# Fused attention and two mixers: where scores and products change from native fp32 to split halves

## The chip, the core and the metric

The kernel runs on one core of a Trainium2 chip. The metric is device time in microseconds. The kernel before takes 890.24 us (median of 3 runs, 889.29 to 891.47); its profiled execution took 888.24 us.

The engines are named as in the profile: PE multiplies matrices (its weight loads are PEld), DVE is the vector engine, ACT the scalar engine, POOL is GpSimd, SP issues most transfers.

## The reference

Three stages follow one another: causal attention over 4 batches, 12 heads, 448 positions and 64 columns; a mixer over positions and then channels; and a second mixer with a cosine and a sine in it.

```
scores = scale * q @ k.T ; scores = where(causal mask, -1e9, scores)
attn   = exp(scores - max) ; attn = attn / (sum(attn) + 1e-9)
x      = attn @ v                                # heads side by side: 768 columns

h  = relu(x.T @ w_tok1) @ w_tok2 ; u = x + h.T   # 448 -> 256 -> 448
x  = u + relu(u @ w_ch1) @ w_ch2                 # 768 -> 1536 -> 768

theta = x @ w_theta ; zr, zi = x * cos(theta), x * sin(theta)
u  = x + w_tok_r @ zr + w_tok_i @ zi
out = u + relu(u @ w_ch)
```

q, k and v are 32-bit floats. The weights reach the kernel as 64-bit floats and are turned into 32-bit ones on the chip.

## The kernel before, in words

Attention runs over 24 pairs of heads (4 batches with 6 pairs each, numbered 0 to 23), each pair in 7 tiles: tile (0, 0) holds the first 64 positions of both heads, and tiles (i, h) for i = 1 to 3 hold 128 queries of head h against 192, 320 or 448 keys. The 168 tiles are the steps of the main loop. `scores` (L332) multiplies q by k into a bank of PSUM, lets DVE add the mask and find the largest value (L356), and lets ACT take the exponential and its sum (L358). Four steps later (`LAG`) `pv` (L384) multiplies the probabilities by v, and after a pair's last tile `finish` (L406) divides by the sums.

Two tables of pair numbers choose how precisely a product is made. A pair in `NATIVE` (L30; pairs 0 to 7) multiplies q and k as they are, in fp32: the 64 rows of each head dimension are loaded into the upper half of a tile and POOL clears the other half (L275). The other pairs load q and k twice over both halves, and ACT and DVE split each into a rounded high part and a rest (L290 to L296): q's high part and rest lie one above the other in `qs`, and `scores` multiplies them by `kh` (L349) and `kl` (L351). A pair in `NATPV` (L31; pairs 0 to 11) has its probabilities transposed by PE (L365), copied by ACT (L367), and multiplied by v in fp32 (L393). The other pairs have the probabilities split into two fp16 halves by ACT and DVE (L376, L378), transposed by a DMA (L381), and multiplied in three fp16 products per block (L403); for these, v is scaled and split too, by `value_squares` and `value_split` (L303, L308), during the pair before.

Beside the pairs runs the conversion of weights. `fetch64` brings a 64-bit tile; `abs64` (L175) lets ACT take the absolute value of the high words with a changed exponent; `round64` (L178) lets DVE shift that left by three (L183), put the sign bit in (L184) and the low word's top bits (L185). 24 large and 4 small tiles are converted at steps given by `ROUNDINGS`; each is then scaled and split by POOL and DVE, and stored. Six tiles (`convert_late`) and the tables of the last mixer (`load_resident`) come later, through the same functions.

From step 53 on, units of the channel mixer (`run_units`, the products at L230 to L232 in `mm3`) are put between the steps by the table `UNIT_STEPS`. A scheduler orders the instructions of each engine; `high_priority` and `issue_after` steer it. Each engine then runs its own list in order, and waits where an operand is missing.

Of the kernel before, what the change touches and what calls it, by code (L numbers as in the profile page):

```python
# [54 lines left out]
def fused(ctx, tc, q, k, v, w_tok1, w_tok2, w_ch1, w_ch2, w_theta, w_tok, w_ch, out):  # L55
# [327 lines left out]

    def pv(pp, i, h):  # L384
        if pp.ps is None:
            pp.ps = bank("pv", 1)
        reg = 0 if i == 0 else ((i - 1) * 2 + h + 1) * D
        pt = pp.pts[i, h]
        if pp.native_pv:
            blks = [8] if i == 0 else [6 + h] + [2 * u + h for u in range(i)]  # L390
            n = D if i == 0 else 2 * D
            for u, vt in enumerate(blks):
                pp.pv = nc.tensor.matmul(pp.ps[:, reg:reg + n], lhsT=pt[:, u], rhs=pp.v[0][:, vt * D:vt * D + n],  # L393
                                 start=(u == 0), stop=(u == len(blks) - 1))
            return
# [10 lines left out]
    def finish(pp, xb, xg):  # L406
        ps, sm = pp.ps, pp.sm
        nc.vector.tensor_scalar(out=sm[:, 0:7], in0=sm[:, 0:7], scalar1=1e-9, scalar2=pp.unit, op0=ALU.add, op1=ALU.mult)
        nc.vector.reciprocal(out=sm[:, 0:7], in_=sm[:, 0:7])
        nc.vector.tensor_tensor(out=xb[:, 1:4, :].rearrange("p i (h d) -> p (i h) d", h=2),  # L410
                                in0=ps[:, D:7 * D].rearrange("p (j d) -> p j d", d=D),
                                in1=sm[:, 0:6].unsqueeze(2).to_broadcast([P, 6, D]), op=ALU.mult)
        for h in range(2):
            r = slice(64 * h, 64 * h + 64)
            nc.vector.tensor_scalar(out=xb[r, 0, 64 * h:64 * h + 64], in0=ps[r, 0:D],
                                    scalar1=sm[r, 6:7], scalar2=None, op0=ALU.mult)
# [570 lines left out]
```

## Time and profile before

| | us |
|---|---|
| median of 3 runs | 890.24 (889.29 to 891.47) |
| profiled execution | 888.24 |
| its span, first to last instruction | 886.5 |
| PE busy | 851.7 (96%) |
| PE weight loads busy | 547.8 (62%) |
| DVE busy | 632.8 (71%) |
| ACT busy | 544.0 (61%) |
| POOL busy | 166.3 (19%) |

Busy time is the union of an engine's instructions. Matmuls overlap, so the time that one takes from the engine is the distance between two starts, not its listed duration; a native fp32 matmul appears as two. The last product of probabilities and v starts at 508.6 us; the second mixer follows.

### The profile page before, as it was taken

What the parts mean: (1) busy time and instruction counts of PE and PEld (TensorE: products, weight loads), DVE (VectorE), ACT (ScalarE), POOL (GpSimd) and SP (SyncE); (2) the same over time, 40 slices, a digit from 0 to 9 for tenths busy, and PEclk for the clock granted to TensorE, in tenths of its full rate; (3) what the DMA queues carried; (4) which work ended last, traced back from release to release, by engine and by line L of the source; (5) the groups of instructions that cost most, each with busy time, mean ns of one, the idle gap of its engine ahead of it and who ended that gap; (6) DMA issues with size and microseconds to landing.
All of it is one profiled execution on the core that took longest, in us unless ns stands there. A gap on an engine that the chain in (4) does not pass through costs nothing.

```text
span 886.5 us, 16065 instructions
## 1 busy us (share of the span) xinstructions
PE 851.7 (96%) x5619; PEld 547.8 (62%) x5619; DVE 632.8 (71%) x1511; ACT 544.0 (61%) x1271; POOL 166.3 (19%) x319
## 2 busy tenths in 40 slices
PE   7999889999899999999999999999999999999998
PEld 6888767776656566565666554555555555555554
DVE  6899996878998775766886258768856448567442
ACT  6798776757776564657655257437746447466441
POOL 2232232223251200121211112051111002101000
PEclk9999989999999999999999999999999999999999
DMA  7857865747899996656565778711622132231011
GB/s 217 255 182 228 289 231 183 272 169 232 205 310 306 288 210 148 165 202 129 162 186 137 232 240 293 238 55 41 201 62 67 50 116 67 69 116 58 18 50 73
DMA packets 105793, 149.63 MB, mean 169 GB/s; under 512 B 61104, under 2 KB 72304, under 8 KB 105712
## 3 DMA queue, kind: packets, MB, share of 16 engines
q1 hardware_dynamic: 105168, 147.59, 55.3%
q0 software_dynamic: 384, 0.79, 0.4%
q8 instruction: 44, 0.72, 0.3%
q14 instruction: 37, 0.30, 0.1%
q10 hardware_dynamic: 160, 0.23, 0.1%
HBM read 112.39 MB, written 22.81 MB: 153 GB/s over the span
## 4 chain that ended last, share of the span: by engine, by line
PE 66%; DVE 13%; DMA 11%; issue 4%; ACT 3%; POOL 1%; SPq 1%; ACTq 0%; DVEq 0%; POOLq 0%
PE ps_mm L230 15%; PE ps_mm L231 15%; PE ps_mm L232 15%; DMA pt<-ph 6%; PE ps_pv L393 3%; PE ps_sc L349 3%; PE ps_sc L230 3%; PE ps_sc L231 3%; PE ps_sc L232 3%; DVE sb L356 2%; DVE ph L378 1%; PE ps_mm L365 1%; DVE wf L184 1%; DMA ws<-w_c 1%; DVE wf L185 1%
## 5 line engine op out<-in xcount | busy, mean ns | idle before, releaser
L230 PE MATMUL ps_mm<-h,ws 128*128 128x448 f16 x432 | 151.9, 353 | 0.4 <-DMA ws<-w_c 0.4
L231 PE MATMUL ps_mm<-h,ws 128*128 128x448 f16 x432 | 152.2, 353 | 0.0
L232 PE MATMUL ps_mm<-h,ws 128*128 128x448 f16 x432 | 152.2, 353 | 0.0
L230 PEld LDWEIGHTS <-ws 128*128 128x128 f16 x720 | 70.4, 98 | 63.4 <-issue 4.1
L232 PEld LDWEIGHTS <-ws 128*128 128x128 f16 x720 | 70.4, 98 | 62.8 <-issue 3.1
L231 PEld LDWEIGHTS <-ws 128*128 128x128 f16 x720 | 70.5, 98 | 62.4 <-issue 4.2
L358 ACT ACTIVATE sb<-sb,mx 128x192 f32<-128x192 f32 (+3 forms) x168 | 89.2, 532 | 32.1 <-DVE mx L356 30.6
L230 PE MATMUL ps_mm<-ut,ws 128*128 128x448 f16 x288 | 102.0, 355 | 5.6 <-ACT ut L160 2.3
L231 PE MATMUL ps_mm<-ut,ws 128*128 128x448 f16 x288 | 102.0, 354 | 0.6 <-DVE ut L196 0.5
L232 PE MATMUL ps_mm<-ut,ws 128*128 128x448 f16 x288 | 102.1, 354 | 0.0
L356 DVE CUSTOM_DVE_ANT_0 sb<-ps_sc,mask 128x192 f32<-128x192 f32 (+3 forms) x168 | 74.3, 456 | 12.7 <-PE ps_mm L365 9.5
L124 ACT ACTIVATE junk<-acc 128x448 bf16<-128x448 f32 x72 | 41.1, 571 | 63.9 <-DVE acc L879 41.0
L160 ACT ACTIVATE ph<-sb 128x192 f16<-128x192 f32 (+3 forms) x84 | 36.4, 442 | 45.9 <-DMA pt<-ph 45.8
L393 PE MATMUL ps_pv<-v_raw,ptf 128*128 128x128 f32 (+1 forms) x456 | 63.9, 277 | 0.3 <-PE ps_mm L138 0.2
L378 DVE SCALAR_TENSOR_TENSOR ph<-sb,ph 128x64 f16<-128x64 f32 (+3 forms) x156 | 44.6, 328 | 26.4 <-ACT ph L160 26.2
L393 PEld LDWEIGHTS ps_pv<-v_raw,ptf 128*128 128x128 f32 x456 | 59.2, 193 | 5.0 <-PE ps_mm L138 1.5
L163 POOL TENSOR_SCALAR h<-t 128x448 f16<-128x448 f32 x48 | 32.8, 685 | 140.3 <-ACT t L477 140.1
L349 PE MATMUL ps_sc<-kh,qs 128*128 128x256 f32 (+2 forms) x112 | 45.9, 416 | 3.3 <-DVE mx L356 3.3
L230 PE MATMUL ps_sc<-th,ut 128*128 128x384 f16 x144 | 46.9, 326 | 0.0
L232 PE MATMUL ps_sc<-th,ut 128*128 128x384 f16 x144 | 46.8, 326 | 0.0
L231 PE MATMUL ps_sc<-th,ut 128*128 128x384 f16 x144 | 46.6, 326 | 0.0
L479 DVE TENSOR_TENSOR h<-t,h 128x448 f16<-128x448 f32 x48 | 30.2, 633 | 19.7 <-POOL h L163 19.5
(215 smaller groups left out, 2040.5 us busy)
## 6 DMA issues: line engine op xcount, KB each, us to landing
ws<-w_c SPq DMA_DIRECT2D x120, 384.0 KB, 4.5
raw<-in_w_ch_dram SPq DMA_DIRECT2D x30, 768.0 KB, 4.5
w_c<-ws SPq DMA_DIRECT2D x30, 384.0 KB, 3.5
q_raw<-in_q_dram SPq DMA_DIRECT2D x16, 448.0 KB, 4.1
k_raw<-in_k_dram SPq DMA_DIRECT2D x16, 448.0 KB, 4.9
v_raw<-in_v_dram SPq DMA_DIRECT2D x24, 288.0 KB, 3.2
x2d<-acc SPq DMA_DIRECT2D x24, 224.0 KB, 3.7
acc<-x2d SPq DMA_DIRECT2D x24, 224.0 KB, 2.8
```

The costliest lines, as they stand in the source:

```text
L124: nc.scalar.activation(j[:, 0:src.shape[-1]], src, AF.Square, accum_out=dst)
L160: nc.scalar.activation(dst, src, AF.Copy, scale=scale)
L163: e.tensor_scalar(out=dst, in0=src, scalar1=scale, scalar2=0.0, op0=ALU.mult, op1=ALU.add)
L230: nc.tensor.matmul(ps, lhsT=ka(a[:, 0]), rhs=kb(b[:, 0]), start=first, stop=False)
L231: nc.tensor.matmul(ps, lhsT=ka(a[:, 0]), rhs=kb(b[:, 1]), start=False, stop=False)
L232: return nc.tensor.matmul(ps, lhsT=ka(a[:, 1]), rhs=kb(b[:, 0]), start=False, stop=last)
L349: nc.tensor.matmul(ps[:, 0:n], lhsT=lhs, rhs=cut(pp.kh), start=True, stop=pp.kl is None)
L356: pp.first = nc.vector.tensor_tensor_reduce(out=dst, in0=src, in1=msk, op0=ALU.add, op1=ALU.min, scale=-0.125, scalar=3.0e38, accum_out=pp ...
L358: pp.last = nc.scalar.activation(sb[:, 0:kk], sb[:, 0:kk], AF.Exp, bias=pp.mx[:, j:j + 1], scale=-1.0, accum_out=pp.sm[:, j:j + 1])
L378: nc.vector.scalar_tensor_tensor(out=dst, in0=sb[:, c0:c1], scalar=PSC, in1=hi[:, c0:c1], op0=ALU.mult, op1=ALU.subtract)
L393: pp.pv = nc.tensor.matmul(pp.ps[:, reg:reg + n], lhsT=pt[:, u], rhs=pp.v[0][:, vt * D:vt * D + n], start=(u == 0), stop=(u == len(blks) - 1))
L479: gates[0] = nc.vector.tensor_tensor(out=t[:, 1], in0=f, in1=t[:, 0], op=ALU.subtract)
```

## The change

Four edits, all in the attention stage and in the conversion of weights:

- `NATIVE` grows to the pairs 0 to 11, and `NATPV` shrinks to 0 to 7. So pairs 8 to 11 turn round: their scores become native, and their probabilities and v are split.
- `abs64` no longer takes the absolute value: ACT copies with the same scale, and POOL multiplies the high words by zero in place, which leaves the sign bit alone. `round64` then shifts and puts the sign in with one DVE instruction instead of two.
- The products of tile (0, 0) are written twice, side by side (`twice`), the sums move by two columns, and `finish` makes all eight blocks of 64 columns with one multiplication. Before it, POOL multiplies a table `own` (a one for the rows of a head, a zero elsewhere) by the factor of tile (0, 0), which takes the place of two instructions of 64 rows. The clearing of a part of `x0` and `x1` is dropped.
- A native product of the last tile is 64 columns wide instead of 128, since the region behind it ends.

```
--- before.py
+++ after.py
@@ -27,8 +27,8 @@
 NEG = -1.0e30
 PSC = 32768.0
 BUFS = dict(ut=12, h2=8, acc=12, ws=8, wf=3, raw=3, sb=3, ph=3, pt=5, t=3, junk=1)
-NATIVE = {0, 1, 2, 3, 4, 5, 6, 7}
-NATPV = {0, 1, 2, 3, 4, 5, 6, 7, 8, 9, 10, 11}
+NATIVE = {0, 1, 2, 3, 4, 5, 6, 7, 8, 9, 10, 11}
+NATPV = {0, 1, 2, 3, 4, 5, 6, 7}
 AHEAD, LAG, LOOK = 500, 4, 2
 KEEP, UBACK = 6, 16
 ROUND_BITS, ROUND_FETCH, ROUND_SPLIT, ROUND_STORE = 1, 2, 3, 5
@@ -173,15 +173,16 @@
         nc.sync.dma_start(out=raw[:, :src.shape[-1]].rearrange("p n w -> p (n w)"), in_=src.bitcast(U32))
 
     def abs64(f, raw):
-        nc.scalar.activation(f, raw[:, :f.shape[-1], 1].bitcast(F32), AF.Abs, scale=REBIAS)
+        high = raw[:, :f.shape[-1], 1].bitcast(F32)
+        nc.scalar.activation(f, high, AF.Copy, scale=REBIAS)
+        product(high, high, 0.0, 1.0)
 
     def round64(f, raw):
 
 
-        low, high = raw[:, :f.shape[-1], 0], raw[:, :f.shape[-1], 1]
+        low, sign = raw[:, :f.shape[-1], 0], raw[:, :f.shape[-1], 1]
         u = f.bitcast(U32)
-        nc.vector.tensor_scalar(out=u, in0=u, scalar1=3, scalar2=None, op0=ALU.logical_shift_left)
-        nc.vector.scalar_tensor_tensor(out=u, in0=high, scalar=0x80000000, in1=u, op0=ALU.bitwise_and, op1=ALU.bitwise_or)
+        nc.vector.scalar_tensor_tensor(out=u, in0=u, scalar=3, in1=sign, op0=ALU.logical_shift_left, op1=ALU.bitwise_or)
         nc.vector.scalar_tensor_tensor(out=u, in0=low, scalar=29, in1=u, op0=ALU.logical_shift_right, op1=ALU.bitwise_or)
 
     def wf_tile():
@@ -239,6 +240,10 @@
     nc.gpsimd.memset(mask, 0.0)
     nc.gpsimd.affine_select(out=mask[:, 320:448], in_=mask[:, 320:448], compare_op=ALU.is_ge, fill=NEG,
                             base=0, pattern=[[-1, P]], channel_multiplier=1)
+    own = ac.tile([P, 2], F32, tag="own", name="own")
+    nc.vector.memset(own, 0.0)
+    for h in range(2):
+        nc.vector.memset(own[64 * h:64 * h + 64, h:h + 1], 1.0)
     mask0 = ac.tile([P, 2, 64], F32, tag="mask0", name="mask0")
     nc.vector.tensor_copy(mask0.rearrange("p a b -> p (a b)"), mask[:, 320:448])
     nc.vector.memset(mask0[64:128, 0, :], NEG)
@@ -262,7 +267,6 @@
     xbufs = []
     for j in range(2):
         xb = ac.tile([P, 4, P], F32, tag=f"x{j}", name=f"x{j}")
-        nc.gpsimd.memset(xb[:, 0, :], 0.0)
         xbufs.append(xb)
 
     loads = {}
@@ -325,7 +329,7 @@
             self.qs, self.kh, self.kl, self.v = parts[:4]
             self.unit = parts[4] if len(parts) > 4 else 1.0
             self.mx = ap2.tile([P, 7], F32, tag="mx", name="mx")
-            self.sm = ap2.tile([P, 8], F32, tag="sm", name="sm")
+            self.sm = ap2.tile([P, 10], F32, tag="sm", name="sm")
             self.pts, self.ps, self.sent = {}, None, None
             self.native_pv = b * NPR + pr in NATPV
 
@@ -356,7 +360,7 @@
         pp.first = nc.vector.tensor_tensor_reduce(out=dst, in0=src, in1=msk, op0=ALU.add, op1=ALU.min, scale=-0.125,
                                        scalar=3.0e38, accum_out=pp.mx[:, j:j + 1])
         pp.last = nc.scalar.activation(sb[:, 0:kk], sb[:, 0:kk], AF.Exp, bias=pp.mx[:, j:j + 1], scale=-1.0,
-                             accum_out=pp.sm[:, j:j + 1])
+                             accum_out=pp.sm[:, 2 + j:3 + j])
         if pp.native_pv:
             nt = 1 + i
             c0 = 64 if i == 0 else 0
@@ -381,16 +385,20 @@
         pp.sent = nc.sync.dma_start_transpose(out=pt[:, 0:nb, :], in_=ph[:, 0:nb * P])
         pp.pts[i, h] = pt
 
+    def twice(ap):
+        return ap.unsqueeze(1).to_broadcast([P, 2, D])
+
     def pv(pp, i, h):
         if pp.ps is None:
             pp.ps = bank("pv", 1)
-        reg = 0 if i == 0 else ((i - 1) * 2 + h + 1) * D
+        reg = 0 if i == 0 else ((i - 1) * 2 + h + 2) * D
         pt = pp.pts[i, h]
         if pp.native_pv:
             blks = [8] if i == 0 else [6 + h] + [2 * u + h for u in range(i)]
-            n = D if i == 0 else 2 * D
             for u, vt in enumerate(blks):
-                pp.pv = nc.tensor.matmul(pp.ps[:, reg:reg + n], lhsT=pt[:, u], rhs=pp.v[0][:, vt * D:vt * D + n],
+                n = 2 * D if reg < 7 * D else D
+                rhs = twice(pp.v[0][:, vt * D:(vt + 1) * D]) if i == 0 else pp.v[0][:, vt * D:vt * D + n]
+                pp.pv = nc.tensor.matmul(pp.ps[:, reg:reg + n], lhsT=pt[:, u], rhs=rhs,
                                  start=(u == 0), stop=(u == len(blks) - 1))
             return
         if i == 0:
@@ -400,20 +408,17 @@
             for u in range(i):
                 jobs += [(1 + u, 0, 2 * u + h), (1 + u, 1, 2 * u + h), (1 + i + u, 0, 2 * u + h)]
         for n, (blk, c, vt) in enumerate(jobs):
-            pp.pv = nc.tensor.matmul(pp.ps[:, reg:reg + D], lhsT=pt[:, blk], rhs=pp.v[c][:, vt * D:(vt + 1) * D],
+            rhs = pp.v[c][:, vt * D:(vt + 1) * D]
+            pp.pv = nc.tensor.matmul(pp.ps[:, reg:reg + (2 * D if i == 0 else D)], lhsT=pt[:, blk], rhs=twice(rhs) if i == 0 else rhs,
                              start=(n == 0), stop=(n == len(jobs) - 1))
 
     def finish(pp, xb, xg):
         ps, sm = pp.ps, pp.sm
-        nc.vector.tensor_scalar(out=sm[:, 0:7], in0=sm[:, 0:7], scalar1=1e-9, scalar2=pp.unit, op0=ALU.add, op1=ALU.mult)
-        nc.vector.reciprocal(out=sm[:, 0:7], in_=sm[:, 0:7])
-        nc.vector.tensor_tensor(out=xb[:, 1:4, :].rearrange("p i (h d) -> p (i h) d", h=2),
-                                in0=ps[:, D:7 * D].rearrange("p (j d) -> p j d", d=D),
-                                in1=sm[:, 0:6].unsqueeze(2).to_broadcast([P, 6, D]), op=ALU.mult)
-        for h in range(2):
-            r = slice(64 * h, 64 * h + 64)
-            nc.vector.tensor_scalar(out=xb[r, 0, 64 * h:64 * h + 64], in0=ps[r, 0:D],
-                                    scalar1=sm[r, 6:7], scalar2=None, op0=ALU.mult)
+        nc.vector.tensor_scalar(out=sm[:, 2:9], in0=sm[:, 2:9], scalar1=1e-9, scalar2=pp.unit, op0=ALU.add, op1=ALU.mult)
+        nc.vector.reciprocal(out=sm[:, 2:9], in_=sm[:, 2:9])
+        product(sm[:, 0:2], own, sm[:, 8:9], 1.0)
+        nc.vector.tensor_tensor(out=xb.rearrange("p i (h d) -> p (i h) d", h=2), in0=ps.rearrange("p (j d) -> p j d", d=D),
+                                in1=sm[:, 0:8].unsqueeze(2).to_broadcast([P, 8, D]), op=ALU.mult)
         pr2 = pp.pr % 2
         c = slice(pr2 * P, (pr2 + 1) * P)
         copy_to(pick("xhi"), xg[0][:, :, c], xb)
```

The first place is the native and split work on PE around the scores of 320 and 448 columns of a pair among 8 to 11. `ptf` are probabilities transposed by PE, `pt` by a DMA; `kh`, `kl`, `qs` are split halves, `k_pad` and `q_raw` native ones. Before:

```order
L349 MATMUL ps_sc<-kh,qs 128x320
L351 MATMUL ps_sc<-kl,qs 128x320
L393 MATMUL ps_pv<-v_raw,ptf 128x128 x3
L365 MATMUL ps_mm<-ident,sb_182 128x128 x2
L393 MATMUL ps_pv<-v_raw,ptf 128x128
L136 LDWEIGHTS ones
L136 MATMUL ps_mm<-tiny,ones 128x1
L138 LDWEIGHTS ones
L138 MATMUL ps_mm<-sqb,ones 128x1
L349 MATMUL ps_sc<-kh,qs 128x448
L351 MATMUL ps_sc<-kl,qs 128x448
L393 MATMUL ps_pv<-v_raw,ptf 128x128 x4
```

And now, where each product has its own weight load:

```order
L412 LDWEIGHTS pt
L412 MATMUL ps_pv<-v_hi,pt 128x64
L412 LDWEIGHTS pt
L412 MATMUL ps_pv<-v_raw,pt 128x64
L412 LDWEIGHTS pt
L412 MATMUL ps_pv<-v_hi,pt 128x64
L353 MATMUL ps_sc<-k_pad,q_raw 128x448 x2
L353 MATMUL ps_sc<-k_pad,q_raw 128x128
L136 LDWEIGHTS ones
L136 MATMUL ps_mm<-tiny,ones 128x1
L412 LDWEIGHTS pt
L412 MATMUL ps_pv<-v_hi,pt 128x64
```

The transposes by PE and the `kl` products are gone from here; runs of fp16 products of 64 columns, three a block, stand between native scores.

The second place is the list of POOL in the first pairs, where the weight tables `ws` are scaled (`g` is a power of two that DVE makes, `raw` the 64-bit words). Before:

```order
L275 MEMSET k_pad_668 64x896
L275 MEMSET q_raw_667 64x896
L130 TENSOR_SCALAR p_w10_141<-g_518 128x1
L130 TENSOR_SCALAR s_514<-g_518 128x1
L163 TENSOR_SCALAR ws_513<-wf_444,s_514 128x768
L130 TENSOR_SCALAR p_w10_141<-g_644 128x1
L130 TENSOR_SCALAR s_640<-g_644 128x1
L163 TENSOR_SCALAR ws_639<-wf_500,s_640 128x768
```

And now:

```order
L279 MEMSET k_pad_668 64x896
L279 MEMSET q_raw_667 64x896
L130 TENSOR_SCALAR p_w10_141<-g_519 128x1
L130 TENSOR_SCALAR raw_405<-raw_405 128x768
L130 TENSOR_SCALAR s_515<-g_519 128x1
L130 TENSOR_SCALAR sm_436<-own_177,sm_436 128x2
L163 TENSOR_SCALAR ws_514<-wf_445,s_515 128x768
L130 TENSOR_SCALAR p_w10_141<-g_645 128x1
L130 TENSOR_SCALAR s_641<-g_645 128x1
L163 TENSOR_SCALAR ws_640<-wf_501,s_641 128x768
```

A sign operation on `raw` stands between the two operations on `g`, and the one on the sums `sm` ahead of the scaling.

The third place is DVE's list at the same tiles: the bits of the weight tile `wf_635` and the sums of pair 2. Before:

```order
L127 TENSOR_SCALAR g_518<-g_518 128x1
L408 TENSOR_SCALAR sm_435<-sm_435 128x7
L409 RECIPROCAL sm_435<-sm_435 128x7
L183 TENSOR_SCALAR wf_635<-wf_635 128x768
L184 SCALAR_TENSOR_TENSOR wf_635<-raw_404,wf_635 128x768
L196 SCALAR_TENSOR_TENSOR ws_513<-wf_444,s_514,ws_513 128x768
L185 SCALAR_TENSOR_TENSOR wf_635<-raw_404,wf_635 128x768
L432 SCALAR_TENSOR_TENSOR h1_543<-ps_mm_544,h1_543 128x256
```

And now:

```order
L127 TENSOR_SCALAR g_519<-g_519 128x1
L417 TENSOR_SCALAR sm_436<-sm_436 128x7
L418 RECIPROCAL sm_436<-sm_436 128x7
L185 SCALAR_TENSOR_TENSOR wf_635<-wf_635,raw_405 128x768
L186 SCALAR_TENSOR_TENSOR wf_635<-raw_405,wf_635 128x768
L197 SCALAR_TENSOR_TENSOR ws_514<-wf_445,s_515,ws_514 128x768
L437 SCALAR_TENSOR_TENSOR h1_543<-ps_mm_544,h1_543 128x256
L437 SCALAR_TENSOR_TENSOR h1_543<-ps_mm_559,h1_543 128x256
```

The tile has two instructions on its bits instead of three, and the first of them reads `raw_405`, which POOL writes. The multiplication that reads POOL's two columns of `sm_436` follows 18 rows behind the reciprocal.

## Rows read from the trace of the kernel before

**Rows 1.** Busy time by stretch: us, each engine, granted clock, DMA share, GB/s
```profile
22.00:110.00 88.00, 83.88 (x602) 72.19 (x599) 81.45 (x208) 72.53 (x197) 25.24 (x41) 1.00 0.74 238
110.00:132.00 22.00, 18.71 (x109) 14.02 (x110) 19.91 (x46) 16.83 (x39) 8.21 (x14) 0.84 0.66 232
132.00:198.00 66.00, 65.99 (x459) 51.20 (x458) 50.41 (x120) 43.38 (x109) 15.96 (x29) 1.00 0.58 206
198.00:264.00 66.00, 61.46 (x462) 40.92 (x460) 63.32 (x162) 49.26 (x120) 24.96 (x42) 1.00 0.87 251
264.00:330.00 66.00, 61.11 (x480) 40.02 (x478) 51.52 (x152) 41.92 (x112) 10.44 (x16) 1.00 1.01 267
330.00:550.00 220.00, 212.31 (x1528) 131.88 (x1527) 146.61 (x380) 125.14 (x303) 35.25 (x73) 1.00 0.67 190
```

**Rows 2.** Timeline of PE in pair 9: start us, us, engine, line
```profile
149.30 0.39 PE L349 MATMUL ps_sc<-kh,qs 128*128 128x320 f32 x1
149.53 0.32 PE L351 MATMUL ps_sc<-kl,qs 128*128 128x320 f32 x1
149.69 0.27 PE L365 MATMUL ps_mm<-ident,sb 128*128 128x128 f32 x1
149.80 1.06 PE L393 MATMUL ps_pv<-v_raw,ptf 128*128 128x128 f32 x8
150.61 0.45 PE L349 MATMUL ps_sc<-kh,qs 128*128 128x448 f32 x1
150.90 0.36 PE L351 MATMUL ps_sc<-kl,qs 128*128 128x448 f32 x1
151.10 0.36 PE L230 MATMUL ps_mm<-ut,ws 128*128 128x448 f16 x1
```

**Rows 3.** Timeline of PE in pairs 1 to 3: native scores and what follows
```profile
24.44 0.49 PE L349 MATMUL ps_sc<-k_pad,q_raw 128*128 128x192 f32 x2
24.77 0.83 PE L393 MATMUL ps_pv<-v_raw,ptf 128*128 128x128 f32 x6
...
30.93 0.92 PE L349 MATMUL ps_sc<-k_pad,q_raw 128*128 128x448 f32 x2
31.68 0.49 PE L365 MATMUL ps_mm<-ident,sb 128*128 128x128 f32 x3
```

**Rows 4.** Timeline of PE around pair 16: ten fp16 products and what follows
```profile
305.31 0.19 PE L403 MATMUL ps_pv<-v_raw,pt 128*128 128x64 f16 x1
...
305.60 0.37 PE L349 MATMUL ps_sc<-kh,qs 128*128 128x256 f32 x1
```

**Rows 5.** Groups by line on DVE: count | busy us, mean ns | idle before
```profile
L378 DVE SCALAR_TENSOR_TENSOR ph<-sb,ph 128x64 f16<-128x64 f32 (+3 forms) x156 | 44.6, 328 | 26.4 <-ACT ph L160 26.2
...
L184 DVE SCALAR_TENSOR_TENSOR wf<-raw,wf 128x768 uint32<-128x768 uint32 (+2 forms) x34 | 33.8, 994 | 0.4
...
L183 DVE TENSOR_SCALAR wf<-wf 128x768 uint32<-128x768 uint32 (+2 forms) x34 | 21.8, 642 | 1.4 <-ACT wf L176 1.4
...
L167 DVE TENSOR_TENSOR qs<-q_raw,qs 64x896 fp32r<-64x896 f32 x16 | 17.9, 1117 | 0.5
...
L415 DVE TENSOR_SCALAR x<-ps_pv,sm 64x64 f32<-64x64 f32 x48 | 13.4, 279 | 0.4
L410 DVE TENSOR_TENSOR x<-ps_pv,sm 128x384 f32<-128x384 f32 x24 | 13.3, 552 | 1.3 <-PE ps_mm L439 0.7 <-PE ps_pv L403 0.4
...
L317 DVE SCALAR_TENSOR_TENSOR v_raw<-v_raw,sv,v_hi 128x576 f16<-128x576 f32 x12 | 11.1, 922 | 1.0 <-POOL v_hi L163 1.0
```

**Rows 6.** Timeline, POOL and DVE at 37 us: start us, us, engine, line
```profile
37.48 1.14 POOL L163 TENSOR_SCALAR ws<-wf,s 128x768 f16<-128x768 f32 x1
...
37.88 1.54 DVE L184 SCALAR_TENSOR_TENSOR wf<-raw,wf 128x768 uint32<-128x768 uint32 x1
```

**Rows 7.** Waits of the whole span: us in total, times, longest
```profile
PEld L403 <- DMA pt<-ph: 9.2, 14, 1.3
...
DVE ws L196 <- POOL ws L163: 6.9, 7, 1.4
```

More of the change, by code (lines that the diff above doesn't have):

```diff
@@ L175, in abs64 @@
     def abs64(f, raw):
-        nc.scalar.activation(f, raw[:, :f.shape[-1], 1].bitcast(F32), AF.Abs, scale=REBIAS)
+        high = raw[:, :f.shape[-1], 1].bitcast(F32)
+        nc.scalar.activation(f, high, AF.Copy, scale=REBIAS)
+        product(high, high, 0.0, 1.0)
     def round64(f, raw):
-        low, high = raw[:, :f.shape[-1], 0], raw[:, :f.shape[-1], 1]
+        low, sign = raw[:, :f.shape[-1], 0], raw[:, :f.shape[-1], 1]
         u = f.bitcast(U32)
-        nc.vector.tensor_scalar(out=u, in0=u, scalar1=3, scalar2=None, op0=ALU.logical_shift_left)
-        nc.vector.scalar_tensor_tensor(out=u, in0=high, scalar=0x80000000, in1=u, op0=ALU.bitwise_and, op1=ALU.bitwise_or)
+        nc.vector.scalar_tensor_tensor(out=u, in0=u, scalar=3, in1=sign, op0=ALU.logical_shift_left, op1=ALU.bitwise_or)
         nc.vector.scalar_tensor_tensor(out=u, in0=low, scalar=29, in1=u, op0=ALU.logical_shift_right, op1=ALU.bitwise_or)
@@ L241, in fused @@
                             base=0, pattern=[[-1, P]], channel_multiplier=1)
+    own = ac.tile([P, 2], F32, tag="own", name="own")
+    nc.vector.memset(own, 0.0)
+    for h in range(2):
+        nc.vector.memset(own[64 * h:64 * h + 64, h:h + 1], 1.0)
     mask0 = ac.tile([P, 2, 64], F32, tag="mask0", name="mask0")
@@ L382, in scores, with twice @@
         pp.pts[i, h] = pt
+    def twice(ap):
+        return ap.unsqueeze(1).to_broadcast([P, 2, D])
     def pv(pp, i, h):
@@ L390, in pv @@
             blks = [8] if i == 0 else [6 + h] + [2 * u + h for u in range(i)]
[L391 removed]
             for u, vt in enumerate(blks):
[L393 removed]
+                n = 2 * D if reg < 7 * D else D
+                rhs = twice(pp.v[0][:, vt * D:(vt + 1) * D]) if i == 0 else pp.v[0][:, vt * D:vt * D + n]
+                pp.pv = nc.tensor.matmul(pp.ps[:, reg:reg + n], lhsT=pt[:, u], rhs=rhs,
                                  start=(u == 0), stop=(u == len(blks) - 1))
@@ L402, in pv @@
         for n, (blk, c, vt) in enumerate(jobs):
-            pp.pv = nc.tensor.matmul(pp.ps[:, reg:reg + D], lhsT=pt[:, blk], rhs=pp.v[c][:, vt * D:(vt + 1) * D],
+            rhs = pp.v[c][:, vt * D:(vt + 1) * D]
+            pp.pv = nc.tensor.matmul(pp.ps[:, reg:reg + (2 * D if i == 0 else D)], lhsT=pt[:, blk], rhs=twice(rhs) if i == 0 else rhs,
                              start=(n == 0), stop=(n == len(jobs) - 1))
@@ L407, in finish @@
         ps, sm = pp.ps, pp.sm
[L408 to L416, printed above, removed]
+        nc.vector.tensor_scalar(out=sm[:, 2:9], in0=sm[:, 2:9], scalar1=1e-9, scalar2=pp.unit, op0=ALU.add, op1=ALU.mult)
+        nc.vector.reciprocal(out=sm[:, 2:9], in_=sm[:, 2:9])
+        product(sm[:, 0:2], own, sm[:, 8:9], 1.0)
+        nc.vector.tensor_tensor(out=xb.rearrange("p i (h d) -> p (i h) d", h=2), in0=ps.rearrange("p (j d) -> p j d", d=D),
+                                in1=sm[:, 0:8].unsqueeze(2).to_broadcast([P, 8, D]), op=ALU.mult)
         pr2 = pp.pr % 2
```

11 lines of the change are left out of this document (5 added, 6 removed).

## The prediction

> **What bounds the kernel now.** I read the stretches first. The table of busy time [rows 1] shows PE at 83.88 of 88 us in the first eight pairs (22 to 110 us), at 65.99 of 66 between 132 and 198 us (pairs 9 to 11), and at 212.31 of 220 us after 330. DVE is close behind: 81.45 of 88 us in the first pairs, 63.32 of 66 in 198 to 264. From 22 to 264 us, which is pairs 2 to 13, the four rows add to 230.0 us of PE (95% of 242) and 215.1 us of DVE (89%). So two engines are near full in the stretch that the change touches: work taken off PE counts only as far as DVE doesn't fill the gap. Beyond 264 us DVE is at 67 to 78% and PE at 93 to 97%. Then I read the price of each product on PE from the timeline, as the time from one start to the next, since matmuls overlap [rows 2 to 4], the DVE groups [rows 5], one place where POOL and DVE meet [rows 6], and the waits [rows 7].
>
> **PE, pairs 8 to 11.** A native product is two passes a matmul. Eight passes start at 149.80 and the next work at 150.61 [rows 2]: 0.10 us a pass. A pair has 18 matmuls of 128 columns and one of 64, so 3.7 us; its 19 transposes cost 0.11 each (149.69 to 149.80), 2.1 us. Both go. In their place come 51 fp16 products; ten of them take 0.29 us [rows 4], so 0.03 each, 1.5 us, and 0.1 for the three of tile 0 that become twice as wide. Saved: 5.8 - 1.6 = 4.2 us a pair, 16.8 in four.
>
> Scores go the other way. Split, a tile costs 0.23 + 0.16 us at 320 columns and 0.29 + 0.20 at 448 [rows 2]; the three tiles that run at 256 columns I price like 320, which is a little high: 3 x 0.39 + 2 x 0.39 + 2 x 0.49 = 2.9 us. Native, one of 192 columns costs 0.33 (24.44 to 24.77) and two of 448 take 0.75 for the two passes of one [rows 3], so 320 lies at 0.54 and 128 at 0.22 by the same slope: 2 x (0.33 + 0.54 + 0.75) + 0.22 = 3.5. That is +0.6 us a pair, +2.4 in four (up to +3 if the 256-wide tiles are cheaper than I took them).
>
> **PE, the rest.** In the eight native pairs the last tile's four matmuls are 64 instead of 128 columns wide: between nothing, if the load of the weights sets the pace, and 0.05 for each pass, 0.4 a pair. I take 0.1. Tile 0 grows by at most 0.1. The pairs 12 to 23 gain 0.1 each from the wider tile 0: +1.2. The two one-column matmuls that find the scale of v are too small to count. Sum on PE: -16.8 + 2.4 + 1.2 = -13.2 us, -14.4 of it before 264 us.
>
> **DVE.** Each weight tile loses its shift L183, 0.64 us [rows 5]; 24 big tiles lie before 264 us, all but a few, so -15.4. The normalisation is one operation in place of 0.55 + 2 x 0.28 = 1.11 us; scaled by columns from the 384-wide one it takes 0.74, so -0.37 a pair, -4.4 over twelve. Pairs 8 to 11 lose two operations of about 1.12 (low parts of q and of k, as many columns each) and gain 13 of 0.33 (156 of them for 12 pairs) and one of 0.92 for v: -2.2 + 4.3 + 0.9 = +3.0 a pair, +12. Sum in this stretch: -8, so 207 of the present 215 us, though it is shifted: out of pairs 2 to 7 and into 8 to 11, where PE was the bound and DVE had room (50.41 of 66 us).
>
> **POOL and the new hand-offs.** POOL gets a sign operation per weight tile. Its nearest row is the 128x768 scaling at 1.14 us [rows 6], with contiguous operands; the new one steps over every second word, so 0.9 to twice that. POOL has room (25.24 of 88 us), so its time is hidden; what counts is whether DVE's first bit operation, which now waits for POOL, comes too soon. In DVE's list the reciprocal stands 18 rows ahead of the multiplication that needs POOL's two columns, so that hand-off is hidden. The sign operation stands behind the power product and ahead of the scale on POOL, and DVE has other work in between. The nearest wait of this kind, DVE's split waiting for POOL's half, is 6.9 us in 7 times over 30 tiles [rows 7], 0.23 a tile. Where the cover is gone, DVE stands for a whole POOL operation, 1.1 us and more. On top, DVE and POOL hold each other up: at 37.88 a bit operation took 1.54 us where L184's mean is 0.99, beside POOL's 1.14 [rows 5, 6]. The bounds of what a tile adds to DVE are thus 0 and 0.55 beside the wait; I take 0.2 for both together, +5 us. DVE then stands at 212 us, hardly less than now.
>
> The Trainium skill ("SBUF — State Buffer", Who interferes with whom) says that a VectorE instruction with two SBUF inputs and a GpSimd one that reads SBUF take one shared port for their whole length, the first blocking the other. The 1.54 us agree in kind: 0.55 more than the mean, beside an operation of 1.14. By that rule the change takes away a one-input operation and leaves two-input ones beside more POOL reads; that is the third rival.
>
> **DMA.** Four more pairs send their probabilities through DMA transposes. PE waited 9.2 us for these in twelve pairs [rows 7], 0.77 a pair, +3 in four; q and k of these pairs come at half the rows, which helps the same queue. The share of DMA in 132 to 198 us was 0.58, so there is room, where 264 to 330 us shows 1.01 [rows 1].
>
> **The sum.** PE work -13.2 and waits for transposes +3; the shorter normalisation and lighter conversion take some idle PE time away in 22 to 132 us (7.4 us idle, all told), of which I count 2. That is -12.2 on the profiled execution's own 888.24 us, which lies 2.0 below the median of the runs. On the median's scale: 890.24 - 12.2, about 878.
>
> **Rivals.**
> 1. DVE takes over in pairs 8 to 11. If 212 us of DVE still fill 89% of their stretch, it lasts 238 us in place of 242: -4, with +1.2 later and some gain from conversions, 886 to 887. For it: DVE at 81.45 of 88 and 63.32 of 66. Against: it reaches 96% in the last of these, and 212 us at 96% would be 221, less than PE needs.
> 2. The relief of DVE in the first pairs frees PE there as well. Idle PE time of 7.4 us in 22 to 132, and in 110 to 132 the granted clock is 0.84, which is 3.5 us of full-rate work lost between the levels 2.4 and 1.2 GHz, after PE had stood idle. Nearly all of it back: -12.2 - 9, 869.
> 3. Slower: POOL in the way of DVE. Each sign operation delays DVE's conversion by its wait or by the port, 0.55 us or more. The point at which DVE's load is no longer lighter is (215 - 207)/24 = 0.33 us a tile; at 0.55 of blocking and as much again of wait, DVE stands at 207 + 26 = 233 us, which at 96% is 243 and at 89% 262, so the stretch is 1 to 20 us longer: 896 by the nearer half. For it: the longest wait of DVE's split for POOL is 1.4 us. Against: there were seven in thirty.
> 4. It cancels: transposes in pairs 8 to 11 bring DMA to the 1.01 that later stretches show, and PE waits away what it saved. Within 2.7 us of now.
>
> **Chances.** The forecast 0.50 (its own range 871 to 884), rival 1 0.16, rival 2 0.18, rival 3 0.10, rival 4 0.06. A difference under 0.3% (2.7 us) can't be told from none. Faster: 0.50 + 0.18 + 0.10 of rival 1 = 0.78; within 0.3%: 0.06 + 0.06 = 0.12; slower 0.10. The range 865 to 889 leaves out most of rival 3 and the low end of rival 2.
>
> **What would show it.** Right: PE's busy time 12 to 14 us lower, the groups of native products at two thirds of their count, L183 gone, DVE between 132 and 198 us well above 76%, the new wait of DVE for POOL under 0.3 us a tile. Wrong: PE idle in pairs 8 to 11 waiting for DVE's maxima or for transposes, DVE's bit operations with a mean over 1.2 us, or a longer stretch at the lower clock.

## The result and the profile after

The changed kernel takes 882.25 us (median of four runs, 880.43 to 884.62) against 889.88 in four runs of the kernel before beside it: a ratio of 0.991 [0.9882 to 0.9938], 7.6 us faster. The profiled execution's span went from 886.5 to 880.5, 6.0 us less. The forecast was 12.2 us.

The page of the kernel after, its first part: busy us, share of the span, instructions.

```profile
PE 840.0 (95%) x5603; PEld 530.6 (60%) x5603; DVE 619.3 (70%) x1462; ACT 539.6 (61%) x1271; POOL 250.3 (28%) x421
```

PE is busy for 11.7 us less (851.7 before), and idle for 40.5 us of its span instead of 34.8. So 5.7 us of what PE saved came back as idle time. Where, the stretches of [rows 1] say, here of the kernel after (same columns; the last three are granted clock, DMA share, GB/s):

```profile
22.00:110.00 88.00, 84.56 (x617) 74.43 (x617) 71.95 (x191) 71.97 (x199) 48.38 (x72) 1.00 0.73 229
110.00:132.00 22.00, 19.62 (x124) 13.56 (x124) 20.40 (x49) 18.28 (x47) 11.62 (x17) 0.92 0.59 183
132.00:198.00 66.00, 58.78 (x428) 37.84 (x427) 56.85 (x154) 43.93 (x113) 30.69 (x45) 0.97 0.99 271
198.00:264.00 66.00, 58.05 (x465) 36.75 (x463) 63.78 (x150) 46.51 (x111) 42.42 (x55) 0.97 0.96 268
264.00:330.00 66.00, 61.87 (x474) 40.79 (x472) 47.33 (x143) 40.08 (x107) 10.35 (x18) 0.97 0.96 258
330.00:550.00 220.00, 215.15 (x1541) 133.06 (x1539) 145.48 (x352) 126.04 (x306) 52.42 (x99) 1.00 0.68 190
```

Idle PE time is a stretch's length less PE's busy time:

| stretch | before | after |
|---|---|---|
| 22 to 132 us | 7.4 | 5.8 |
| 132 to 264 us | 4.6 | 15.2 |
| 264 to 550 us | 12.6 | 9.0 |
| the rest of the span | 10.2 | 10.5 |

All of the loss lies between 132 and 264 us, and there two columns changed. DVE went from 50.41 to 56.85 of 66 us in the first half, as it was meant to. The DMA share went from 0.58 and 0.87 to 0.99 and 0.96, near the 1.01 that 264 to 330 us showed before. A share can pass 1 (1.14 in the last section), so it doesn't say by itself that nothing more would go through. The stretches are equal times, not equal work.

The waits of the kernel after (us in total, times, longest), first those of PE and of its weight loads, which show the same pauses a second time and are not added to PE's, then DVE's for POOL (the third line is the start of the kernel, where PE waited 4.8 us for the mask before):

```profile
PE ps_pv L412 <- DMA pt<-ph: 11.7, 11, 4.0
PE ps_sc L353 <- DVE mx L360: 6.9, 7, 1.7
PE ps_sc L353 <- DMA k_pad<-in_k_dram: 5.0, 1, 5.0
...
PEld L412 <- DMA pt<-ph: 14.0, 11, 4.2
...
DVE wf L185 <- POOL raw L130: 6.3, 10, 0.9
...
DVE ws L197 <- POOL ws L163: 4.2, 4, 1.7
```

Before, the weight loads waited 9.2 us for the transposes [rows 7], and PE itself these:

```profile
PE ps_pv L403 <- DMA pt<-ph: 6.1, 10, 1.2
...
PE ps_sc L349 <- DVE mx L356: 4.0, 8, 1.0
```

PE's waits for transposed probabilities grew by 5.6 us, those for DVE's maxima by 2.9. PE's own waits in 132 to 264 us alone, first the kernel before, then the one after:

```profile
PE ps_pv L403 <- DMA pt<-ph: 2.2, 4, 0.9
...
```

```profile
PE ps_pv L412 <- DMA pt<-ph: 7.7, 10, 1.5
PE ps_sc L353 <- DVE mx L360: 3.8, 3, 1.7
...
```

Before, no wait for maxima is listed there. So of the 10.6 us of idle time that came in this stretch, 5.5 are waits for transposes, 3.8 for maxima and 1.3 for other things.

The chain of work that ended last in 132 to 264 us, followed back from one instruction to what released it, by line, first of the kernel before, then of the one after:

```profile
by line: issue 14.9%; PE ps_pv L393 8.1%; PE ps_mm L230 7.7%; PE ps_mm L232 7.5%; PE ps_mm L231 7.4%; DVE ph L378 4.3%; PE ps_mm L365 3.8%; DVE sb L356 3.5%; DVE ut L196 2.8%; POOL ws L163 2.6%; DVE wf L184 2.4%; PE ps_mm L429 2.4%; PE ps_s
```

```profile
by line: DMA pt<-ph 34.3%; DMA q_raw<-in_q_dram 9.2%; issue 6.3%; PE ps_mm L231 5.4%; DMA ws<-w_c 5.4%; PE ps_mm L232 4.9%; ACT junk L124 4.8%; PE ps_mm L233 4.7%; ACT ph L160 3.8%; DVE ph L382 3.7%; DVE qs L167 2.0%; ACT sb L362 1.9%; ACT 
```

Before, PE's own lines lead and no DMA is among the twelve listed. After, transposes are 34.3% of the 132 us, and with the loads of q and of scaled weights half of the chain is transfers. It is one chain of one execution, and its shares don't set the time: in the run with a fourth buffer, at the end of the experiments, transposes are 13.3% of the same chain, and the time is the same.

The DVE groups that answer to [rows 5] (count | busy us, mean ns | idle before). L186 is the one for L184, L185 has taken in the shift of L183, and L420 replaces L410 and L415:

```profile
L382 DVE SCALAR_TENSOR_TENSOR ph<-sb,ph 128x64 f16<-128x64 f32 (+3 forms) x208 | 63.8, 351 | 34.0 <-ACT ph L160 33.4
L186 DVE SCALAR_TENSOR_TENSOR wf<-raw,wf 128x768 uint32<-128x768 uint32 (+2 forms) x34 | 34.0, 1001 | 0.1
...
L185 DVE SCALAR_TENSOR_TENSOR wf<-wf,raw 128x768 uint32<-128x768 uint32 (+2 forms) x34 | 31.7, 932 | 6.4 <-POOL raw L130 6.3
...
L420 DVE TENSOR_TENSOR x<-ps_pv,sm 128x512 f32<-128x512 f32 x24 | 16.4, 685 | 0.6 <-PE ps_pv L412 0.4
...
L321 DVE SCALAR_TENSOR_TENSOR v_raw<-v_raw,sv,v_hi 128x576 f16<-128x576 f32 x16 | 15.0, 937 | 0.0
```

### The profile page after: what moved, and what is told of

The parts are those of the page before. It is cut to its first block, busy times and chain, and to the rows that moved or that the text cites. A ratio compares the mean times of both kernels' runs of the same rounds, so it can differ in the third digit from the quotient of the medians.

```text
span 880.5 us, 16257 instructions
## 1 busy us (share of the span) xinstructions
PE 840.0 (95%) x5603; PEld 530.6 (60%) x5603; DVE 619.3 (70%) x1462; ACT 539.6 (61%) x1271; POOL 250.3 (28%) x421
## 4 chain that ended last, share of the span: by engine, by line
PE 66%; DMA 13%; DVE 8%; ACT 6%; issue 3%; POOL 2%; SPq 0%; ACTq 0%; POOLq 0%; DVEq 0%
PE ps_mm L231 15%; PE ps_mm L232 15%; PE ps_mm L233 15%; DMA pt<-ph 7%; PE ps_sc L353 4%; PE ps_pv L401 2%; PE ps_sc L231 2%; PE ps_sc L233 2%; PE ps_sc L232 2%; DMA ws<-w_c 2%; ACT junk L124 2%; PE ps_pv L412 1%; DVE ut L197 1%; DMA q_raw<-in_q_dram 1%; ACT sb L362 1%
## 5 line engine op out<-in xcount | busy, mean ns | idle before, releaser
L362 ACT ACTIVATE sb<-sb,mx 128x320 f32<-128x320 f32 (+3 forms) x168 | 89.3, 533 | 27.3 <-DVE mx L360 26.8
L382 DVE SCALAR_TENSOR_TENSOR ph<-sb,ph 128x64 f16<-128x64 f32 (+3 forms) x208 | 63.8, 351 | 34.0 <-ACT ph L160 33.4
L160 ACT ACTIVATE ph<-sb 128x192 f16<-128x192 f32 (+3 forms) x112 | 48.2, 440 | 58.2 <-DMA pt<-ph 57.8
L360 DVE CUSTOM_DVE_ANT_0 sb<-ps_sc,mask 128x320 f32<-128x320 f32 (+3 forms) x168 | 74.1, 455 | 13.6 <-PE ps_mm L369 9.5
L353 PE MATMUL ps_sc<-k_pad,q_raw 128*128 128x192 f32 (+3 forms) x168 | 58.2, 446 | 8.5 <-DMA k_pad<-in_k_dram 5.0
L759 POOL TENSOR_SCALAR tmp<-tmp 128x384 f32<-128x384 f32 x28 | 15.5, 554 | 146.2 <-ACT tmp L758 143.2
L412 PE MATMUL ps_pv<-v_hi,pt 128*128 128x64 f16 (+1 forms) x512 | 35.5, 194 | 11.7 <-DMA pt<-ph 11.7
L484 DVE TENSOR_TENSOR h<-t,h 128x448 f16<-128x448 f32 x48 | 32.3, 677 | 19.3 <-POOL h L163 19.2
```

The source lines that it names most:

```text
L160: nc.scalar.activation(dst, src, AF.Copy, scale=scale)
L353: nc.tensor.matmul(ps[:, 0:n], lhsT=lhs, rhs=cut(pp.kh), start=True, stop=pp.kl is None)
L360: pp.first = nc.vector.tensor_tensor_reduce(out=dst, in0=src, in1=msk, op0=ALU.add, op1=ALU.min, scale=-0.125, scalar=3.0e38, accum_out=pp ...
L362: pp.last = nc.scalar.activation(sb[:, 0:kk], sb[:, 0:kk], AF.Exp, bias=pp.mx[:, j:j + 1], scale=-1.0, accum_out=pp.sm[:, 2 + j:3 + j])
L382: nc.vector.scalar_tensor_tensor(out=dst, in0=sb[:, c0:c1], scalar=PSC, in1=hi[:, c0:c1], op0=ALU.mult, op1=ALU.subtract)
L412: pp.pv = nc.tensor.matmul(pp.ps[:, reg:reg + (2 * D if i == 0 else D)], lhsT=pt[:, blk], rhs=twice(rhs) if i == 0 else rhs, start=(n == 0 ...
```

## The experiments

Two kinds of theory stood against each other: that PE's work sets the time (A) and that DVE's load, the transposes or another wait does (B, D, T). Each run was timed beside the kernel before; ratios are to that kernel, and "idle" is the span less PE's busy time. Small differences of ratios between builds are read with care: every edit also gives the scheduler another order.

**Parts alone and parts undone.** First the kernel before with the two tables of pair numbers alone.

```diff
-NATIVE = {0, 1, 2, 3, 4, 5, 6, 7}
-NATPV = {0, 1, 2, 3, 4, 5, 6, 7, 8, 9, 10, 11}
+NATIVE = {0, 1, 2, 3, 4, 5, 6, 7, 8, 9, 10, 11}
+NATPV = {0, 1, 2, 3, 4, 5, 6, 7}
```

> Only the two tables change: pairs 8 to 11 get native scores and split products; conversion and normalisation stay as before. Theory A (the work taken off PE is what pays, DVE only limits it): 884 to 887 us, 3 to 6 below before, since the 3 us a pair that DVE gains in pairs 8 to 11 meet a conversion that is not lightened. Theory B (what pays is the lighter load on DVE, the tables by themselves only move work): 888 to 892 us.

Measured 1.0004 [0.9986 to 1.0021], PE busy 843.4, idle 46.5. Its stretches from 132 to 264 us:

```profile
132.00:198.00 66.00, 57.40 (x415) 38.44 (x416) 55.41 (x152) 39.09 (x104) 19.13 (x29) 0.95 1.00 253
198.00:264.00 66.00, 53.90 (x420) 34.20 (x418) 62.99 (x164) 44.76 (x112) 30.38 (x48) 0.95 0.87 251
```

PE's work fell by 8.3 us and its idle time rose by 11.7: alone, the tables gain nothing. That is B's range, not A's. Next the lighter conversion alone (the new `abs64` and `round64` in the kernel before):

```diff
-        nc.scalar.activation(f, raw[:, :f.shape[-1], 1].bitcast(F32), AF.Abs, scale=REBIAS)
+        high = raw[:, :f.shape[-1], 1].bitcast(F32)
+        nc.scalar.activation(f, high, AF.Copy, scale=REBIAS)
+        product(high, high, 0.0, 1.0)
...
-        nc.vector.tensor_scalar(out=u, in0=u, scalar1=3, scalar2=None, op0=ALU.logical_shift_left)
-        nc.vector.scalar_tensor_tensor(out=u, in0=high, scalar=0x80000000, in1=u, op0=ALU.bitwise_and, op1=ALU.bitwise_or)
+        nc.vector.scalar_tensor_tensor(out=u, in0=u, scalar=3, in1=sign, op0=ALU.logical_shift_left, op1=ALU.bitwise_or)
```

> Only the conversion of weights changes: sign by POOL, two DVE instructions on the bits instead of three. Theory A: 887 to 889.5 us, 0 to 3 below before, because PE is the bound where DVE is relieved and only its idle time in the first pairs can shrink. Theory B: 882 to 885 us. A third reading, POOL in the way of DVE: over 891 us, with the bit operations at a mean over 1.2 us.

Measured 0.9956 [0.9939 to 0.9973]: 3.9 us, with DVE at 620.8 (632.8 before) and idle at 31.8. This lies between the two ranges. The new normalisation alone (the third and fourth edits of the change, put into the kernel before):

```diff
-        nc.vector.tensor_tensor(out=xb[:, 1:4, :].rearrange("p i (h d) -> p (i h) d", h=2),
...
+        nc.vector.tensor_tensor(out=xb.rearrange("p i (h d) -> p (i h) d", h=2), in0=ps.rearrange("p (j d) -> p j d", d=D),
```

> Only the normalisation changes: tile 0 written twice, one multiplication a pair, POOL's two columns before it. Theory A: 888.5 to 891 us, no difference that can be told (DVE saves 0.4 us a pair, PE gains 0.1 in the split pairs). Theory B: 886 to 888 us. POOL in the way: over 892, with DVE idle before the multiplication waiting for POOL.

0.9978 [0.9959 to 0.9997], 2.0 us, hardly clear of none, and on the edge between the two ranges. And the kernel after with the old tables, so both of these without the tables:

```diff
-NATIVE = {0, 1, 2, 3, 4, 5, 6, 7, 8, 9, 10, 11}
-NATPV = {0, 1, 2, 3, 4, 5, 6, 7}
+NATIVE = {0, 1, 2, 3, 4, 5, 6, 7}
+NATPV = {0, 1, 2, 3, 4, 5, 6, 7, 8, 9, 10, 11}
```

> The changed kernel with the old tables: light conversion and one normalisation, native scores in pairs 0 to 7, native products in pairs 0 to 11. Conversion alone gave 0.9956 and normalisation alone 0.9978, together 0.993 if they add. Theory D: 884 to 886 us, the tables being worth 2 to 4 us on a DVE that the other edits have relieved by some 25 us. Rival T: 881 to 883, the tables worth nothing here too.

0.9983 [0.9964 to 1.0002], a miss for both theories: the two gains don't add (3.9 and 2.0 alone, 1.5 together, on 612.6 us of DVE). The last of these is the kernel after with the old conversion:

```diff
-        nc.scalar.activation(f, high, AF.Copy, scale=REBIAS)
-        product(high, high, 0.0, 1.0)
+        nc.scalar.activation(f, raw[:, :f.shape[-1], 1].bitcast(F32), AF.Abs, scale=REBIAS)
...
```

> The changed kernel with the old conversion of weights (absolute value on ACT, three DVE instructions on the bits). Theory A, with DVE as the limit: 883 to 886 us, 1 to 4 above the changed kernel, PE idle in pairs 8 to 11 longer than in the changed kernel. Theory B: 888 us or more, the whole gain gone. If PE alone bounds the stage: the same as the changed kernel within 1 us.

0.9973 [0.9956 to 0.9991], idle 42.8, between the ranges of A and B and nearer to B's. So the conversion is worth 0.0063 of the time, 5.6 us, when the tables are in, and the tables 0.0073, 6.5 us, when conversion and normalisation are in (0.991 against 0.9983), against nothing without. Apart the two halves of the change gain 0 and 1.5 us, together 7.6.

**PE's work alone.** The kernel before, in which the native products of pairs 8 to 11 take only the first block of each tile; the other blocks' products are left out, their transposes not.

```diff
+            if 8 <= pp.b * NPR + pp.pr:
+                blks = blks[:1]
```

> The kernel before, where the native pairs 8 to 11 multiply only the first block of each tile's probabilities with v and leave the other 12 products of a pair out. PE has 10.6 us less to do (96 passes of 0.11 us) in the stretch that the tables touch, and no other engine has a different load. Theory D: 887 to 891 us, at most 3 below before. Theory A: 879 to 882 us.

0.9901 [0.9882 to 0.9921], 8.8 us on 7.0 us of PE busy time less (844.7, where 10.6 less was expected), idle 35.3 against 34.8 before. With the DMA share at 0.70 and 0.81 in the two stretches, work taken from PE is passed on in full. A stands where nothing else is added; that DVE alone bounds these pairs falls.

**DVE's load alone.** The kernel before without the last bit operation of the conversion; the low words' top three bits are left out.

```diff
-        nc.vector.scalar_tensor_tensor(out=u, in0=low, scalar=29, in1=u, op0=ALU.logical_shift_right, op1=ALU.bitwise_or)
```

> The kernel before, with the last DVE instruction of each weight conversion left out (the low words' top three bits are not put in). It takes 1.0 us per large tile off DVE, 24 of them before 264 us, and changes nothing on PE, POOL or the queues. Theory D (DVE bounds the stretch up to about 265 us, so that work taken off PE there turns into idle time): 879 to 884 us. Theory A (PE is the bound there): 886 to 889 us.

0.984 [0.9811 to 0.9869], 14.2 us, the largest gain of all and more than D expected, with PE busy 851.9 as before:

```profile
PE 851.9 (97%) x5619; PEld 548.9 (63%) x5619; DVE 591.1 (67%) x1451; ACT 543.3 (62%) x1271; POOL 162.7 (19%) x319
```

41.7 us less on DVE take idle PE time from 34.8 to 25.2; the two profiled executions differ by 9.4 us in their spans, less than the 14.2 of the timed runs. The same edit with the two tables added:

```diff
-NATIVE = {0, 1, 2, 3, 4, 5, 6, 7}
+NATIVE = {0, 1, 2, 3, 4, 5, 6, 7, 8, 9, 10, 11}
...
-        nc.vector.scalar_tensor_tensor(out=u, in0=low, scalar=29, in1=u, op0=ALU.logical_shift_right, op1=ALU.bitwise_or)
```

> The kernel before with the two changed tables and the same DVE instruction left out as in the run beside it. Its distance from that run is what the tables are worth where DVE has room; on the unrelieved kernel they were worth nothing (ratio 1.0004). Theory D: 6 to 12 us below its neighbour, near the 8 us that PE's own instructions become cheaper by. Rival T (the transposes by DMA and the stretches at the lower clock eat what PE saves): within 2 us of its neighbour.

0.9859 [0.9825 to 0.9893]. PE's busy time fell by another 12.3 us (839.6), idle rose to 39.1, and nothing was gained over the run before:

```profile
132.00:198.00 66.00, 61.55 (x463) 41.79 (x461) 56.63 (x162) 45.19 (x118) 20.88 (x34) 0.93 0.94 273
198.00:264.00 66.00, 56.94 (x440) 36.64 (x439) 60.44 (x164) 45.68 (x112) 28.30 (x45) 0.97 1.00 280
```

DVE has less to do over the whole run (599.9 us) and the tables still give nothing, beside a DMA share of 0.94 and 1.00 and waits of PE for transposes of 8.3 us (3.6 without the tables). That speaks for the transposes, T, as what the tables run into; but in the two stretches themselves DVE still stands at 56.63 and 60.44 of 66 us. It also sits badly with the pair of runs above, where the tables gave 6.5 us on a DVE that was relieved by less (612.6 us): what they are worth does not grow with DVE's room alone.

**Scores and products apart.** The kernel after, products split in pairs 8 to 11 but scores as before:

```diff
-NATIVE = {0, 1, 2, 3, 4, 5, 6, 7, 8, 9, 10, 11}
+NATIVE = {0, 1, 2, 3, 4, 5, 6, 7}
```

> The changed kernel with native scores in pairs 0 to 7 alone, so in pairs 8 to 11 scores, q and k are split again and only the products change from the kernel before. Against the changed kernel PE saves about 4 us (split scores are cheaper) and DVE has 2.2 us a pair more, 9 in all, ACT 1.9 a pair. Theory D: 884 to 888 us, 2 to 6 above the changed kernel. Theory A: 878 to 880 us.

1.0032 [1.001 to 1.0054], a little slower than before, where both theories expected a gain, though PE is as little busy (840.9) as after. Idle is 50.0, and PE waits for transposes 17.1 us. Its first stretch of the two:

```profile
132.00:198.00 66.00, 57.59 (x450) 40.06 (x449) 62.34 (x156) 45.17 (x115) 34.22 (x44) 0.95 0.97 267
```

Then scores native in pairs 8 to 11 but products as before:

```diff
-NATPV = {0, 1, 2, 3, 4, 5, 6, 7}
+NATPV = {0, 1, 2, 3, 4, 5, 6, 7, 8, 9, 10, 11}
```

> The changed kernel with native products in pairs 0 to 11 as before, so of the tables only the scores of pairs 8 to 11 change. Against the changed kernel PE has about 16 us more work and DVE about 21 us less. Theory D (DVE's load up to 265 us sets the time): 875 to 880 us, 2 to 7 below the changed kernel. Theory A (PE's work sets it): 890 us or more.

0.9985 [0.9972 to 0.9998], nearer to A's 890 than to D's range. PE busy 854.0, idle 31.7:

```profile
132.00:198.00 66.00, 64.17 (x419) 47.97 (x418) 41.23 (x96) 38.24 (x97) 22.35 (x37) 1.00 0.54 181
```

With conversion and normalisation lightened, the four corners are: neither 0.9983, scores alone 0.9985, products alone 1.0032, both 0.991. In the first stretch native scores take DVE from 62.34 to 56.85 us beside split products; they do not pay by themselves, as PE is at 64.17 of 66 with DVE at 41.23, and split products do not pay without them. They go together.

**Two attempts to get more.** Native scores in pairs 0 to 15 and native products up to 11:

```diff
-NATIVE = {0, 1, 2, 3, 4, 5, 6, 7, 8, 9, 10, 11}
-NATPV = {0, 1, 2, 3, 4, 5, 6, 7}
+NATIVE = {0, 1, 2, 3, 4, 5, 6, 7, 8, 9, 10, 11, 12, 13, 14, 15}
+NATPV = {0, 1, 2, 3, 4, 5, 6, 7, 8, 9, 10, 11}
```

> The changed kernel with native products in pairs 0 to 11 and native scores in pairs 0 to 15. Against the run beside it PE gains some 4 us and DVE loses 2.2 us a pair, 9 in all, in the stretch from 198 to 264 us where it is 96% busy. Theory D: 869 to 876 us, below its neighbour by 2 to 8. Theory A: 2 to 5 above its neighbour.

0.9986 [0.9972 to 1.0], a miss: DVE is down to 594.1 and idle to 28.7, but PE's busy time is up to 857.4. And the kernel after with a fourth buffer for the split probabilities, since ACT waits 57.8 us (45 times) for transposes to free one:

```diff
-BUFS = dict(ut=12, h2=8, acc=12, ws=8, wf=3, raw=3, sb=3, ph=3, pt=5, t=3, junk=1)
+BUFS = dict(ut=12, h2=8, acc=12, ws=8, wf=3, raw=3, sb=3, ph=4, pt=5, t=3, junk=1)
```

> The changed kernel with four buffers for the split probabilities instead of three. ACT waited 57.8 us for a transpose to free one of them. Rival T (the chain through the transposes holds pairs 8 to 14 up): 876 to 880 us, and ACT's wait falls by half or more. Theory D: within 2 us of the changed kernel.

0.9905 [0.9886 to 0.9923], the changed kernel's own time. Its waits and stretches:

```profile
PE ps_sc L353 <- DVE mx L360: 8.7, 8, 1.9
PE ps_pv L412 <- DMA pt<-ph: 5.0, 7, 2.4
```

```profile
132.00:198.00 66.00, 57.75 (x422) 36.94 (x421) 57.45 (x162) 44.59 (x119) 29.11 (x43) 0.97 1.01 273
198.00:264.00 66.00, 57.78 (x459) 37.43 (x458) 63.41 (x147) 44.72 (x106) 35.63 (x52) 0.97 0.98 263
```

PE's wait for transposes fell from 11.7 to 5.0 us, yet PE is as idle in these stretches as in the changed kernel (16.5 us against 15.2). The wait only moved, to the maxima and to many small ones, with DVE and DMA still as full. ACT's own wait for the buffer fell only from 57.8 to 51.8 us, not by half, so a fourth buffer hardly relieved it. No run is clearly faster than the changed kernel except the two that leave bits out.

## Why the prediction was right, and where it was too large

The direction was right, and so was the first step: PE's work falls. But only half of that reaches the end on the profile (6.0 of 11.7 us), and by the runs above it reaches it only together with the relief of DVE. By the sum of the prediction the tables alone would have gained some 11 us (-16.8 + 2.4 + 3) and the relief 2; alone the tables gained nothing. That the total came as near as it did is thus in part luck. By steps:

- **PE's work** (-13.2 forecast): busy time -11.7. Pairs 8 to 11 gave up their native products, a third of all, as forecast. The groups of native products and of the transposes on PE stand at 304 and 152 where they had 456 and 228:

```profile
L401 PE MATMUL ps_pv<-v_raw,ptf 128*128 128x128 f32 (+1 forms) x304 | 41.5, 276 | 1.1 <-DVE x L420 0.8 <-ACT ptf L371 0.2
...
L369 PE MATMUL ps_mm<-ident,sb 128*128 128x128 f32 x152 | 24.5, 276 | 0.0
```

  Counted from each matmul's start to the next one's, or to its own end where PE then stands idle, which adds up to the busy time, both together fell by 26.0 us and split products rose by 8.3, against 23.2 and 7.6 in the working. The scores cost +2.4, as forecast, though two of the new native ones ran at the lower clock (last section), which cost 0.84 and 0.53 us. All other matmuls, which the change doesn't touch, took 3.6 us more, which is where the gap to the forecast of -13.2 lies.
- **DVE** (212 us forecast in 22 to 264 us): 71.95 + 20.40 + 56.85 + 63.78 = 213.0. Its parts hold too: L183 is gone, the normalisation takes 685 ns where 740 was worked out, and the split of v 937 for 922. Between 132 and 198 us DVE is at 86%.
- **POOL and the hand-offs** (0.2 us a tile for wait and contention): the wait is 6.3 us over 34 tiles, 0.19, the longest 0.9, and the bit operations' means are 0.93 and 1.00 us, not over 1.2. Rival 3 did not come. Not foreseen: 6.2 us more at the bits of the 14 small weight tiles `wkf`, which the forecast left out. The port rule of the Trainium skill ("SBUF — State Buffer", Who interferes with whom) has the right sign here, but in few places: POOL's busy time rose by 84 us, and DVE's L382 went from 328 to 351 ns, all of it in the operations of 64 columns (235 to 285 ns; those of 128, 256 and 384 columns stayed at 305, 418 and 551). Of those of 64 columns after the change, the 36 that overlap a POOL instruction in the trace take 393 ns in the mean, the other 60 take 220. L184's successor takes 1001 ns against 994, so in the conversion blocking for a whole operation is not what the mean shows.
- **Idle PE time in the first pairs** (-2): -1.6 in 22 to 132 us.
- **Waits for transposes** (+3): this is the term that was too small. Priced at 0.77 us a pair from later pairs, they rose by 4.8 in the row that it was priced by (9.2 to 14.0) and by 5.6 in PE's own, and idle time between 132 and 264 us rose by 10.6. 3.8 us of that are waits for DVE's maxima, which the sum had no term for at all. The sentence it rested on, that a DMA share of 0.58 left room, took the room for enough: 0.42 + 0.13 of 66 us, 36 us, and the change used all but 3 of it. That the wait was hidden in the later pairs by PE's other work, while here PE had just been relieved, is a reading that no run tests. In 132 to 264 us there are now 40 transposes instead of 17, and the median one takes longer:

```profile
pt<-ph SPq DMA_TRANSPOSE x17, 3.9
```

```profile
pt<-ph SPq DMA_TRANSPOSE x40, 4.8
```

  (before and after, in this stretch: count, median us from issue to landing). The loads of 64-bit weights beside them went from 5.2 to 6.6 us. Over the whole run the median of the transposes rose only from 3.5 to 3.8, and PE's longest wait for one, 4.0 us instead of 1.2, lies behind this stretch (last section). This is rival 4 in its mechanism, at about half its size: 5.7 of 11.7 us came back as idle time. In the run with the tables alone, and in the one without native scores in pairs 8 to 11, it took all.
- **The clock**: not in the forecast. After the change four stretches of about 3.5 us ran near the 1.2 GHz level where there was one twice as long (last section), some 3.3 us more; that is inside the busy time of the first step.

The sum of the measured terms: -11.7 of busy time, +5.7 of idle, -6.0 on the profile (the 5.7 are 10.6 between 132 and 264 us, -1.6 ahead of them, -3.6 behind them up to 550 us, and 0.3 elsewhere). The 2 us of idle time that was to be won back in the first pairs and the 3 for transposes missed the change's main interaction. The relief of DVE is worth more than I let it be: 14.2 us for 41.7 on DVE, with no change on PE. And without any relief the work that the tables save turns into waits.

Open is which of the two nearly full resources holds PE in 132 to 264 us: in every run with split products there DMA stands at 0.87 to 1.01 and DVE at 55 to 64 of 66 us, a fourth buffer only moved the wait from the one to the other, and no run lightened the DMA traffic alone. Open too is why conversion and normalisation don't add (3.9 and 2.0 alone, 1.5 together); POOL's higher load could take it back, which is only argued. And open is why the tables are worth nothing, 6.5 us and again nothing on kernels with 632.8, 612.6 and 591.1 us of DVE. No run changed the order of the instructions alone, so how much of a difference of a few us comes from the order that the scheduler chose is not known.

## What to carry to other kernels

Before taking work off the busiest engine, look at how full the second and the third are in that same stretch, DMA among them, and price what the edit puts on them by the room that is left there, not by the mean wait of another stretch. A wait that costs little beside a full engine may cost more once that engine has been relieved: here it was priced at 3 us and came to 5.5 between 132 and 264 us, with 3.8 for maxima that had no price. Edits that gain next to nothing alone can gain together (0 and 1.5 us apart, 7.6 together), so test them in pairs, in a table of four.
